# Moving three bursts of work by one step in a cosformer-attention and Swish-MLP kernel

## The chip, the cores and the metric

The kernel runs on one core of a Trainium2 chip. The metric is the device time of one execution in microseconds (us). The time before is a median of three runs. The profile is one execution on the same chip, taken apart from the timed ones. Its span, 275.6 us, runs from the first to the last recorded instruction and is shorter than the device time of that execution (277.38 us).

## What is computed

There are 8 batches of 8 heads, 576 positions and 64 features. For each batch and head:

```
r = relu(x)                                 # for q and for k
phi(x) = [r * cos(theta), r * sin(theta)]   # theta = pi/2 * position / 576
kv  = phi(k)^T v        z = sum over positions of phi(k)
att = (phi(q) kv) / (phi(q) z + 1e-6)
```

The heads are laid side by side, which gives 4608 tokens of 512 features. These go through a two-layer network with 2048 hidden features:

```
h = x @ w_in ;  g = h * sigmoid(beta * h) ;  out = g @ w_out
```

All inputs and outputs are fp32. The kernel multiplies in bf16.

## The kernel before, in words

The tokens are handled in nine chunks of 512, the attention in eight batches of 576 positions. A batch of attention is always computed inside the chunk before the one that needs it. The order of the work is written out by hand: every engine runs its instructions in the order in which the Python code emits them, and only waits on results hold one back.

**Chunk 0** is the loop over 32 slots at L783. Slots 0 to 15 make one group of 128 hidden features each: four matmuls of 512 columns, and one Swish on ScalarE (`h_group`). Slots 16 to 31 multiply by w_out: slots 16 to 23 call `o_part(0, tt, part)`, which takes one token tile and four hidden groups; slots 24 to 31 take one hidden group for all four token tiles, `o_mm(0, tt, (slot - 16,))`. Each of these slots is four matmuls of 512 columns. Slot 24 reads row 8 of the bf16 weights, `wout[:, 8]`, slot 25 row 9, and so on. A row is made by `cast_out(j)`, on VectorE, or on ScalarE where the call has `"a"`: it copies one row from the fp32 staging tile and divides by beta.

After its matmuls, a slot calls what the dictionary `early` (L736) has for it. These are the bursts of the second batch (b = 1):

- slot 4, `rest()`: emits the VectorE work that later slots find in the queue, last of all `v_scale(1, 0)`, `k_relu(1)`, and the two halves of `q_relu` for batch 1, which need the transfer of raw q;
- slot 22: the keys-values product `kv_mm` (72 small matmuls into banks 6 and 7), and its copy `kv_take` on ScalarE;
- slot 23, `second()` (L720): 18 transposes of q on TensorE (`q_turn_pe`), then copies of them (`takes`) shared between ScalarE and VectorE, with `cast_out(8)` to `cast_out(15)` mixed in;
- slots 25 and 26, `num_seven`: the numerators, with their division on VectorE; slot 25 has `cast_out(13)` too;
- slots 28 and 29, `x_turn_pe`: the transposes of the result, and their copies.

**Chunk 1** is the loop at L811: 16 slots of `h_group(1, slot)`. Between them lie the preparations for batch 2. `v_half(2, 1, n0, n1)` multiplies positions n0 to n1 - 1 (of nine) of v by the sine: slots 3 to 8 do pieces 3 to 8 on ScalarE, slot 4 does pieces 0 to 2 on VectorE. `w_sums` (slot 6) makes four sums of weight blocks on VectorE. `kv_all(2)` (slot 11) is the keys-values product and its copy on VectorE, followed by the multiplication of q by the tangent (`tan_mul`), also on VectorE. Chunk 1 ends with the products of w_out, which use a fast scheme with seven block products for eight (`o_fast`, L536), and reads `kv` in `num_all(2, ...)` there.

**Chunk 2** (L1013 with c = 2) works likewise and ends with a list of product calls: `y["1"]`, `y["5"]` and so on are eight-step matmul products on TensorE, `y["c1"]` and the like are copies, `y["a2"]`, `y["a7"]`, `y["a3"]` are additions on VectorE. Product "4" is accumulated in the same bank (`b_ps`) that addition "a7" reads. `x_sums(3)` and `wh_sums(12)` are VectorE sums of inputs and of weights for the fast scheme of chunk 3.

Of the kernel before, what the change touches and what calls it, by code (L numbers as in the profile page):

```python
# [17 lines left out]
NQ = 9  # L18
# [4 lines left out]
def kernel(  # L23
# [93 lines left out]
    def cast_out(j, eng="d"):  # L117
        i, jj = divmod(j, 4)
        st = stages["out", i]
        if eng == "a":  # L120
            nc.scalar.activation(wout[:, j, :], st[:, jj, :], AF.Copy, scale=rbeta[:, j : j + 1])
        else:
            nc.vector.tensor_scalar(wout[:, j, :], st[:, jj, :],
                                    scalar1=rbeta[:, j : j + 1], scalar2=None, op0=ALU.mult)
# [138 lines left out]
    def kv_out(jp, bank):  # L263
        return ps[:, bank : bank + 2, jp * 2 * E : (jp + 1) * 2 * E]

    def kv_mm(b, jp, bank, jjs=(0, 1)):
        t = kv_out(jp, bank)
        for n in range(NQ):
            for jj in jjs:
                for g in range(2):  # L270
                    hs = slice(g * HP, (g + 1) * HP)
                    nc.tensor.matmul(  # L272
                        t[jj * HP : (jj + 1) * HP, g], lhsT=rk[hs, n, 2 * jp + jj, :],
                        rhs=vb[hs, n, 2 * jp + jj].rearrange("q s e -> q (s e)"),
                        start=(n == 0), stop=(n == NQ - 1))

    def kv_take(jps, bank, eng="dve"):
        a0, a1 = jps[0], jps[-1] + 1
        o = kv[:, :, a0:a1].rearrange("q g s c e -> q g (s c e)")
        a = ps[:, bank : bank + 2, a0 * 2 * E : a1 * 2 * E]  # L280
        if eng == "act":
            nc.scalar.copy(o, a)
        else:
            nc.vector.tensor_copy(o, a)
# [14 lines left out]
    def x_rden(bank, slot, n0, n1, jps):  # L299

        w, m = len(jps), n1 - n0
        nv = ps[:, bank : bank + 2, slot * E : (slot + w * m) * E].rearrange("q j (i s e) -> q j i s e", s=w, e=E)
        den = small.tile([P, 2, m, w], FP32, name="den", tag=f"den{m}{w}")
        nc.vector.tensor_tensor(  # L304
            den, nv[:, :, :, :, D],
            eps9[:, n0:n1].unsqueeze(1).unsqueeze(3).to_broadcast([P, 2, m, w]), op=ALU.add)
        rden = small.tile([P, 2, m, w], FP32, name="rden", tag=f"rden{m}{w}")
        nc.vector.reciprocal(rden, den)
        return nv, rden, n0, jps

    def x_mul(got, n0, n1):
        nv, rden, first, jps = got
        a, z, w = n0 - first, n1 - first, len(jps)
        o = xs[:, n0:n1, jps[0] : jps[-1] + 1].rearrange("q n s (j d) -> q j n s d", j=2)
        nc.vector.tensor_tensor(  # L315
            o.rearrange("q j n s d -> q j (n s) d"),
            nv[:, :, a:z, :, 0:D].rearrange("q j n s d -> q j (n s) d"),
            rden[:, :, a:z].rearrange("q j n s -> q j (n s)").unsqueeze(3).to_broadcast([P, 2, (z - a) * w, D]),
            op=ALU.mult)
# [27 lines left out]
    def x_turn_pe(b, n0, n1, bank, engs=("act",), jps=(0, 1)):  # L347
        m, w = n1 - n0, len(jps)
        tv = ps[:, bank].bitcast(BF16)[:, 0 : w * m * P].rearrange("q (n s c) -> q n s c", n=m, s=w)
        for i in range(m):  # L350
            for s_, jp in enumerate(jps):
                nc.tensor.matmul(tv[:, i, s_, :], lhsT=xs[:, n0 + i, jp, :], rhs=ident, is_transpose=True,  # L352
                                 start=(i == 0 and s_ == 0), stop=(i == m - 1 and s_ == w - 1))
        for k_, (c, o, a, z) in enumerate(pieces(b, n0, n1)):
            dst, src = xt_tile(c)[:, o : o + z - a, jps[0] : jps[-1] + 1], tv[:, a - n0 : z - n0]
            if engs[k_ % len(engs)] == "act":
                nc.scalar.copy(dst, src)
            else:
                nc.vector.tensor_copy(dst, src)
# [80 lines left out]
    def wh_sums(jt):  # L440
        f0 = jt % 4
        A11, A12, A21, A22 = (win[jt // 4][:, 2 * jp : 2 * jp + 2, f * P : (f + 1) * P]
                              for f in (f0, f0 + 1) for jp in range(2))
        s1, s2, s3, s4 = (w_sum(jt, i) for i in range(4))
        nc.vector.tensor_tensor(s1, A21, A22, op=ALU.add)
        nc.vector.tensor_tensor(s3, A11, A21, op=ALU.subtract)
        nc.vector.tensor_tensor(s2, s1, A11, op=ALU.subtract)
        return nc.vector.tensor_tensor(s4, A12, s2, op=ALU.subtract)
# [265 lines left out]
    def num_seven(jp, bank):  # L714
        for n in range(7):
            num_mm(1, n, jp, bank, n)
# [3 lines left out]
    def second():  # L720

        takes.append(q_turn_pe(1, 0, 4, hold=True))
        takes.append(q_turn_pe(1, 1, 6, hold=True))
        cast_out(8)
        takes[0]("act", 0)
        takes[0]("dve", 1)
        cast_out(9, "a")
        takes[0]("dve", 0)
        takes[0]("act", 1)
        cast_out(10)  # L730
        for e, i in (("act", 0), ("dve", 1), ("act", 1), ("dve", 0)):
            takes[1](e, i)
        for j in (11, 12, 14, 15):
            cast_out(j, "a")
# [1 line left out]
    early = {  # L736
        4: lambda: (num_mm(0, 8, 0, 2, 0), num_mm(0, 8, 1, 2, 1), rest()),
        15: lambda: v_scale(1, 1, eng="act"),
        22: lambda: (kv_mm(1, 0, 6), kv_mm(1, 1, 6), kv_take((0, 1), 6, "act")),
        23: second,  # L740
        25: lambda: (num_seven(0, 4), x_mul(x_rden(4, 0, 0, 7, (0,)), 0, 7), cast_out(13)),
        26: lambda: (num_seven(1, 6), x_mul(x_rden(6, 0, 0, 7, (1,)), 0, 7)),
        28: lambda: x_turn_pe(1, 0, 7, 4, ("act",), (0,)),
        29: lambda: x_turn_pe(1, 0, 7, 5, ("dve",), (1,)),
    }

    def num_rest():
# [14 lines left out]
    def v_half(b, cs, n0=0, n1=NQ, eng="dve"):  # L762
        if b >= B:
            return
        v_scale(b, cs, n0=n0, n1=n1, eng=eng)
        if cs == 1 and n1 == NQ and b + 1 < B:
            load_raw(b + 1, "v")
# [3 lines left out]
        if b + 1 < B:  # L771
            load_raw(b + 1, "k")

    def kv_all(b, bank=6):
        kv_mm(b, 0, bank)
        kv_mm(b, 1, bank)
        kv_take((0, 1), bank)

    def x_part(b, t, bank):
        x_div(t, bank)  # L780
# [30 lines left out]
    for slot in range(16):  # L811
        h_group(1, slot)
        if slot == 0:
            num_rest()
            att_q(2)
            v_half(2, 0)
        if 3 <= slot < NQ:
            v_half(2, 1, slot, slot + 1, "act")
        if slot == 4:
            k_all(2)  # L820
            v_half(2, 1, 0, 3)
        elif slot == 6:
            w_sums()
        elif slot == 11:
            kv_all(2)
            for jp in range(2):
                tan_mul(nc.vector, qs_of(2)[:, jp], qts[0][:, jp], 0, NQ)
    q_relu(3, 0, "act")
# [184 lines left out]
    for c in range(2, NTC):  # L1013
        b = c + 1
        parts = (6, 0, 4) if c < FAST else (0, 6, 4)
        xb, yb = ((2, 3, 6), (1 if c == FAST - 1 else 7, 3, 6)) if c < FAST else ((3, 2, 0), (1, 2, 0)) if b < B else ((0, 3, 6), (1, 3, 6) if c + 1 < NTC else (1, 4, 7))
        x, y = o_fast(c, 0, xb), o_fast(c, 1, yb)
        if c >= FAST:
            chunk(c, b, x, y, parts)
            continue  # L1020
        sums = h_first(c)
        for t, bank in enumerate(parts):
            num_all(b, t, bank)
        q_tan(b + 1, 0, sums)
        q_tan(b + 1, 1)
        for i, n in enumerate("156273"):
            x[n]()
            if n in "156":
                x["c" + ("u" if n == "6" else n)]()
                x_part(b, i, parts[i])  # L1030
        for j in range(4):
            k_piece(b + 1, j)
        for n in ("a7", "a2", "a3"):
            x[n]()
        att_q(b + 2, False)
        y["1"]()
        y["c1"]()
        v_half(b + 1, 1, 0, 1, "act")
        x["4"]()
        x["c4"]()  # L1040
        v_half(b + 1, 1, 1, 2, "act")
        v_half(b + 1, 0, 0, 5)
        y["5"]()
        y["c5"]()
        if c == FAST - 1:
            x_sums(c + 1)
            wh_sums(12)
        v_half(b + 1, 1, 2, 3, "act")
        y["6"]()
        y["cu"]()  # L1050
        y["2"]()
        y["a2"]()
        y["7"]()
        y["a7"]()
        v_half(b + 1, 0, 5, 7)
        y["3"]()
        y["a3"]()
        v_half(b + 1, 0, 7, 9)
        v_half(b + 1, 1, 3, 9, "act")
        y["4"]()  # L1060
        y["c4"]()
        q_turn_dma(b + 2)
# [30 lines left out]
```

## Time and profile before

| | before |
|---|---|
| time, median of 3 | 278.01 us (277.81 to 278.37) |
| span of the profiled execution | 275.6 us |
| TensorE matmuls | 268.9 us busy, 98% |
| VectorE | 221.0 us, 80% |
| ScalarE | 184.6 us, 67% |
| GpSimd | 67.8 us, 25% |
| TensorE clock granted | 1.00 |

The busy time of TensorE includes modelled matmul ends, so short idle times between two matmuls are better read from the start times in the timeline. The chain of waits goes back from the last instruction to what released each step; it says which engine set the end, piece by piece. In the timeline a row is a run of like instructions: start, length, engine, source line, operation, output and input tile, count, and in brackets how long the engine had been idle before and what ended that.

A 512-column matmul of chunk 0 starts 0.216 us after the one before it (eight of them from 41.28 us on take 1.89 us, the last of them 0.379 us), so a slot of four takes 0.87 us.

### The profile page before, as it was taken

Reading aid. Unit: us, or ns where it says so; the run is one execution under the profiler, and the core shown is the slowest. Engines: PE = TensorE matmul, PEld = TensorE weight load, DVE = VectorE, ACT = ScalarE, POOL = GpSimd, SP = SyncE. Lnnn points to the kernel's source line nnn. Section 1 sums busy time; section 2 is a strip of 40 time slices with the busy share of each in tenths; the row PEclk is TensorE's granted clock in tenths of the full one; section 3 lists DMA queues with packets and bytes.
Section 4 is the critical chain, followed back from the end, with each engine's and each line's share of the span. In section 5 each row is a group of like instructions: output and inputs, shape, how many; then the busy total and the mean of one; then the engine's idle time right before and its main releaser. Section 6 shows DMA issues by size and latency. Waiting matters only on the chain.

```text
span 275.6 us, 9047 instructions
## 1 busy us (share of the span) xinstructions
PE 268.9 (98%) x3749; PEld 199.8 (73%) x3749; DVE 221.0 (80%) x578; ACT 184.6 (67%) x381; POOL 67.8 (25%) x87
## 2 busy tenths in 40 slices
PE   8899999999999999999999999999999999999993
PEld 8554455446875599869866998688768886888683
DVE  5989968599999898599959995899589589558851
ACT  5778757797248657697669756976694289429821
POOL 1444000600087073106420552044300140000000
PEclk9999999999999999999999999999999999999999
DMA  7999999999969999961899199915400640033005
GB/s 248 369 394 382 393 389 312 375 193 377 244 153 309 245 309 295 394 130 38 179 359 267 39 220 301 121 21 107 114 2 12 117 115 2 0 70 86 2 24 130
DMA packets 50745, 54.00 MB, mean 196 GB/s; under 512 B 31232, under 2 KB 31760, under 8 KB 50704
## 3 DMA queue, kind: packets, MB, share of 16 engines
q1 hardware_dynamic: 47744, 45.88, 59.5%
q0 software_dynamic: 2688, 7.34, 8.9%
q8 instruction: 29, 0.48, 0.7%
q10 hardware_dynamic: 272, 0.21, 0.3%
q14 instruction: 12, 0.10, 0.2%
HBM read 36.71 MB, written 9.44 MB: 167 GB/s over the span
## 4 chain that ended last, share of the span: by engine, by line
PE 83%; DMA 12%; DVE 2%; ACT 1%; SPq 1%; issue 0%; ACTq 0%; DVEq 0%
PE ps L547 35%; PE ps L468 16%; PE ps L422 13%; PE ps L380 10%; DMA raw_q<-in_q_dram 7%; DMA w_stage<-in_moe_w_in_dram 5%; PE ps L293 4%; PE ps L517 3%; PE ps L272 2%; DVE win L115 1%; ACT vb L217 1%; SPq L79 1%; PE ps L234 0%; PE ps L352 0%; DVE qb L194 0%
## 5 line engine op out<-in xcount | busy, mean ns | idle before, releaser
L413 ACT ACTIVATE g_t<-ps,beta 128x512 bf16<-128x512 f32 x96 | 61.0, 698 | 3.1 <-DVE ps L498 2.8
L547 PEld LDWEIGHTS <-S 128*128 128x128 bf16 x589 | 51.3, 98 | 5.0
L510 POOL DMA_DIRECT2D out_dram<-o_sb x56 | 33.5, 604 | 66.3 <-ACT o_sb L523 24.6
L380 PE MATMUL ps<-xt,win 128*128 128x512 bf16 (+1 forms) x196 | 42.8, 375 | 0.1
L547 PEld LDWEIGHTS <-g_t 128*128 128x128 bf16 x440 | 38.2, 98 | 4.3 <-issue 0.3
L422 PE MATMUL ps<-xt,win 128*128 128x512 bf16 (+1 forms) x184 | 40.8, 351 | 0.0
L388 ACT ACTIVATE g_t<-ps,beta 128x512 bf16<-128x512 f32 x48 | 32.2, 690 | 8.0 <-PE ps L380 7.8
L380 PEld LDWEIGHTS <-win 128*128 128x128 bf16 x196 | 18.8, 98 | 21.0 <-issue 0.4
L547 PE MATMUL ps<-wout,g_t 128*128 128x256 bf16 (+1 forms) x284 | 31.7, 262 | 0.0
L547 PE MATMUL ps<-wout,S 128*128 128x256 bf16 (+1 forms) x305 | 31.5, 255 | 0.0
L547 PE MATMUL ps<-T,S 128*128 128x256 bf16 (+1 forms) x284 | 30.8, 262 | 0.0
L399 DVE TENSOR_TENSOR S<-g_t 128x512 bf16<-128x512 bf16 (+1 forms) x66 | 25.1, 409 | 3.6 <-ACT g_t L413 2.7
L217 ACT ACTIVATE vb<-raw_v,sin 128x256 bf16<-128x256 f32 (+1 forms) x61 | 27.4, 501 | 0.9 <-DMA raw_v<-in_v_dram 0.9
L222 POOL TENSOR_TENSOR qs<-qt,tanr 128x1152 bf16<-128x1152 bf16 x6 | 14.2, 2382 | 50.8 <-DVE den L304 29.8
L468 PEld LDWEIGHTS <-w_stage 128*128 128x128 bf16 x224 | 21.6, 98 | 6.7
L468 PE MATMUL ps<-w_stage 128*128 128x256 bf16 x168 | 26.2, 272 | 0.0
L422 PEld LDWEIGHTS <-win 128*128 128x128 bf16 x184 | 17.9, 98 | 10.1
L315 DVE TENSOR_TENSOR xs<-ps,rden 128x768 bf16<-128x768 f32 (+4 forms) x26 | 22.8, 883 | 0.8
L219 DVE TENSOR_SCALAR vb<-raw_v,cos 128x256 bf16<-128x256 f32 x63 | 20.5, 380 | 0.1
L468 PEld LDWEIGHTS <-win 128*128 128x128 bf16 x168 | 16.4, 98 | 4.8 <-issue 0.3
L468 PE MATMUL ps<-xt,win 128*128 128x256 bf16 x112 | 19.1, 273 | 0.0
L594 ACT COPY p<-ps 128x256 f32<-128x256 f32 x16 | 6.0, 373 | 17.0 <-PE ps L547 16.9
(105 smaller groups left out, 417.6 us busy)
## 6 DMA issues: line engine op xcount, KB each, us to landing
raw_v<-in_v_dram SPq DMA_DIRECT2D x7, 1152.0 KB, 9.9
raw_k<-in_k_dram SPq DMA_DIRECT2D x7, 1152.0 KB, 7.5
raw_q<-in_q_dram SPq DMA_DIRECT2D x7, 1152.0 KB, 7.7
out_dram<-o_sb POOLq DMA_DIRECT2D x56, 128.0 KB, 4.4
w_stage<-in_moe_w_in_dram SPq DMA_DIRECT2D x3, 1024.0 KB, 13.0
w_stage<-in_moe_w_out_dram SPq DMA_DIRECT2D x2, 1024.0 KB, 8.1
w_stage<-in_moe_w_out_dram SPq DMA_DIRECT2D x4, 512.0 KB, 11.9
out_dram<-o_sb SPq DMA_DIRECT2D x12, 128.0 KB, 2.4
```

What stands on the lines that cost most here:

```text
L217: nc.scalar.activation(o, a, AF.Copy, scale=t[:, n : n + 1])
L219: nc.vector.tensor_scalar(o, a, scalar1=t[:, n : n + 1], scalar2=None, op0=ALU.mult)
L222: return eng.tensor_tensor(dst.rearrange("q n (g p) -> q n g p", g=2), src.rearrange("q n (g p) -> q n g p", g=2), tanr[:, n0:n1].unsqueez ...
L315: nc.vector.tensor_tensor(o.rearrange("q j n s d -> q j (n s) d"), nv[:, :, a:z, :, 0:D].rearrange("q j n s d -> q j (n s) d"), rden[:, :, ...
L380: nc.tensor.matmul(ps[:, h_bank(c, jt), i * 64 : (i + w) * 64], lhsT=win[jt // 4][:, mi, (jt % 4) * P : (jt % 4 + 1) * P], rhs=xt[:, i : i ...
L388: nc.scalar.activation(gs[c, jt // 4][:, jt % 4], ps[:, h_bank(c, jt)], AF.Silu, scale=beta[:, jt : jt + 1])
L399: return nc.vector.tensor_tensor(o, l, r, op=op)
L413: nc.scalar.activation(gs[c, jt // 4][:, jt % 4], ps[:, bank], AF.Silu, scale=beta[:, jt : jt + 1])
L422: nc.tensor.matmul(ps[:, bank, o * 64 : z * 64], lhsT=win[jt // 4][:, mi, (jt % 4) * P : (jt % 4 + 1) * P], rhs=xt[:, o:z, jp, g * HP : (g ...
L468: nc.tensor.matmul(dst, lhsT=left[:, g], rhs=right[:, :, g * HP : (g + 1) * HP], start=start and g == 0, stop=stop and g == 1, skip_group_ ...
L510: (eng or own).dma_start(out=out_v[bb, n][:, m0:m1], in_=o_sb[hf * HP : (hf + 1) * HP, m0:m1])
L547: nc.tensor.matmul(dst[:, m : m + w], lhsT=left(i), rhs=right[:, i, m : m + w], start=start and i == 0, stop=stop and i == order[-1], skip ...
```

## The change

There are three moves. They are meant to place each burst nearer to the time at which its inputs are there and its engine is free.

1. **Chunk 0, second batch.** Each burst comes one slot later: keys-values from slot 22 to 23, `second` from 23 to 24, the numerators from 25 and 26 to 26 and 27, the transposes of the result from 28 and 29 to 29 and 30. The purpose is to give the raw transfers of batch 1 one more slot to arrive. Since slot 24 reads `wout[:, 8]`, `cast_out(8)` can no longer stand in `second`; it is emitted with the keys-values burst in slot 23.
2. **Chunk 1, keys-values.** `kv_all(2)` comes in slot 10 in place of 11, and its copy is done by ScalarE in place of VectorE. For the sine pieces to be ready sooner, VectorE makes five of them (0 to 4) and ScalarE four (5 to 8), in slots 2 to 5.
3. **Chunk 2, the sums.** `wh_sums(12)`, four VectorE additions, moves from ahead of the additions `y["a2"]`, `y["a7"]`, `y["a3"]` to behind them.

```
         takes.append(q_turn_pe(1, 0, 4, hold=True))
         takes.append(q_turn_pe(1, 1, 6, hold=True))
-        cast_out(8)
         takes[0]("act", 0)
         takes[0]("dve", 1)
         cast_out(9, "a")
...
-        22: lambda: (kv_mm(1, 0, 6), kv_mm(1, 1, 6), kv_take((0, 1), 6, "act")),
-        23: second,
-        25: lambda: (num_seven(0, 4), x_mul(x_rden(4, 0, 0, 7, (0,)), 0, 7), cast_out(13)),
-        26: lambda: (num_seven(1, 6), x_mul(x_rden(6, 0, 0, 7, (1,)), 0, 7)),
-        28: lambda: x_turn_pe(1, 0, 7, 4, ("act",), (0,)),
-        29: lambda: x_turn_pe(1, 0, 7, 5, ("dve",), (1,)),
+        23: lambda: (kv_mm(1, 0, 6), kv_mm(1, 1, 6), kv_take((0, 1), 6, "act"), cast_out(8)),
+        24: second,
+        26: lambda: (num_seven(0, 4), x_mul(x_rden(4, 0, 0, 7, (0,)), 0, 7), cast_out(13)),
+        27: lambda: (num_seven(1, 6), x_mul(x_rden(6, 0, 0, 7, (1,)), 0, 7)),
+        29: lambda: x_turn_pe(1, 0, 7, 4, ("act",), (0,)),
+        30: lambda: x_turn_pe(1, 0, 7, 5, ("dve",), (1,)),
...
-    def kv_all(b, bank=6):
+    def kv_all(b, bank=6, eng="dve"):
         kv_mm(b, 0, bank)
         kv_mm(b, 1, bank)
-        kv_take((0, 1), bank)
+        kv_take((0, 1), bank, eng)
...
-        if 3 <= slot < NQ:
-            v_half(2, 1, slot, slot + 1, "act")
+        if 2 <= slot < 6:
+            v_half(2, 1, slot + 3, slot + 4, "act")
         if slot == 4:
             k_all(2)
-            v_half(2, 1, 0, 3)
+            v_half(2, 1, 0, 5)
         elif slot == 6:
             w_sums()
-        elif slot == 11:
-            kv_all(2)
+        elif slot == 10:
+            kv_all(2, eng="act")
...
         if c == FAST - 1:
             x_sums(c + 1)
-            wh_sums(12)
         v_half(b + 1, 1, 2, 3, "act")
...
         v_half(b + 1, 0, 7, 9)
+        wh_sums(12)
         v_half(b + 1, 1, 3, 9, "act")
```

## The prediction

> **What bounds the kernel now.** I read the page first. Its row of busy times leaves TensorE as the only candidate:
>
> ```profile
> PE 268.9 (98%) x3749; PEld 199.8 (73%) x3749; DVE 221.0 (80%) x578; ACT 184.6 (67%) x381; POOL 67.8 (25%) x87
> ```
>
> At 98% no transfer or other engine can be worth much except where TensorE stands still, so next I went through the chain of waits in order of time and looked for pieces that are not TensorE's. From 40 us to the end there is one such stretch ahead of the last microsecond. These are the two places (start, length, what):
>
> ```profile
> 24.45 14.81 DMA raw_q<-in_q_dram
> 39.26 0.02 issue
> 39.28 0.77 DVE qb L194
> 40.05 0.05 issue
> 40.10 1.34 PE ps L234 x18
> 41.44 1.73 PE ps L517 x8
> ...
> 107.43 0.05 DVEq L599
> 107.48 0.21 issue
> 107.69 0.42 DVE o_sb L599
> 108.11 0.04 issue
> 108.16 1.05 PE ps L547 x15
> ```
>
> The reader is to see two things. Raw q of batch 1 lands at 39.26, VectorE takes its relu, and TensorE's transposes start 0.05 us after the first half of that. At 108.16 TensorE waits for a VectorE addition. Between 41 and 105 us TensorE sets the pace, so **every microsecond lost or won on TensorE in either place goes into the total**. The third look is the timeline around 40 us:
>
> ```profile
> 39.01 1.04 PE L517 MATMUL ps<-wout,g_t 128*128 128x512 bf16 x4
> 39.28 1.43 DVE L194 TENSOR_SCALAR qb<-raw_q 128x1152 bf16<-128x1152 f32 x2 [1.64 <-DMA raw_q<-in_q_dram]
> ...
> 40.59 0.69 ACT L239 COPY qt<-ps 128x640 bf16<-128x640 bf16 x1 [0.50 <-PE ps L234]
> 40.64 0.48 DVE L123 TENSOR_SCALAR wout<-w_stage,rbeta 128x512 bf16<-128x512 f32 x1
> ...
> 41.18 0.72 ACT L121 ACTIVATE wout<-w_stage,rbeta 128x512 bf16<-128x512 f32 x1
> ...
> 41.28 1.89 PE L517 MATMUL ps<-wout,g_t 128*128 128x512 bf16 x8
> ```
>
> Here `cast_out(8)` is the VectorE row at 40.64, directly behind q's relu, and `cast_out(9)` the ScalarE row at 41.18, behind the first copy of the transposes. They end at 41.12 and 41.90. Slots 24 and 25 (the x8) start at 41.28 and 42.15, just behind them: the 18 transposes lie in TensorE's order ahead of slot 24 and give both casts time.
>
> **What the Trainium skill says.** "PSUM — Partial Sum Buffer", section "Engine vs sequencer instructions": ScalarE's and VectorE's queues are strict FIFO, and matmuls start in program order, with weight loads alone pulled ahead. The trace agrees: VectorE sits idle for 1.64 us for raw q with `cast_out(8)` behind it in the queue. The same page, section "PSUM bank collisions raise a hardware error": instructions of two engines on one bank are kept apart, reads against reads included. Here ScalarE's copy at 43.48 came 0.51 us late, after VectorE's tangent product on the same bank. The working below rests on both.
>
> **Part 1, chunk 0.** Nothing is added or removed; the order changes. What it wins: slot 23's last matmul starts at 39.01 + 3 x 0.216 = 39.66, so TensorE could go on at 39.88 and starts the transposes at 40.10, a wait of 0.22; the second nine wait 0.16 to 0.18 for the second half of q (weight load at 40.76, "0.16 <-DVE qb" in the rows of weight loads). That is 0.40 us.
>
> What it loses, step by step. TensorE now runs slot 23 at 37.78 (28 matmuls from 31.72), keys-values at 38.7 to 39.9, and then wants slot 24. But slot 24 reads the row of `cast_out(8)`. That call has moved only behind the keys-values burst in the code; on VectorE it is still behind q's relu, which was emitted in slot 4. It cannot end before 41.12. So slot 24 starts at 41.12 + 0.05 = 41.17 and TensorE idles 1.3 us, with the transposes queued behind it although their q is there at 40.71.
> Slot 24 takes 4 x 0.216 = 0.87, so the transposes start at 42.04. ScalarE's first copy waits for them, and `cast_out(9)` is queued behind that copy. Before, the cast ended at 41.90, which is 1.80 behind the transposes' start at 40.10. With the same lag it ends at 43.84, and slot 25 starts at 43.89. The transposes are over at about 43.0, so TensorE idles 0.87 a second time. Before, slot 25 started at 42.15 with the same work done: **+1.74 us, in which the 0.40 won is already counted**.
> Slot 26 follows at 44.76; its `cast_out(10)`, on VectorE behind two tangent products of 0.70 each from about 42.8, ends at 44.6 and costs nothing. The numerators (0.58) bring TensorE to 46.3. Slot 27 needs `cast_out(11)`: behind the copies of the second nine transposes, which alternate between two engines on one bank, I get 45.2 + 0.48 + 0.71 = 46.42, so slot 27 starts at 46.47, another 0.17. Slot 28 would start at 47.33 + 0.65 for the second numerators = 48.0, against 46.09 before. Sum for part 1: **+1.9 us**. After slot 28 the casts lead: `cast_out(13)` ends at about 48.5, slot 29 starts at 48.9. The result's last copy (0.62, starting 0.59 after its transposes) has only slot 31 (0.87) and the transposes' 0.4 to hide in, and ends just in time for chunk 1.
> The bounds: if only the first wait is real, +0.87 (the transposes' 0.98 us less the 0.11 that slot 24 starts earlier). If the copies run without gaps, 1.7; if the alternation slips by one more copy (0.59), 2.5.
>
> **Part 2, chunk 1.** VectorE loses the keys-values copy (0.69) and gains two sine pieces (three took 0.87 from 57.91, so 0.58): -0.11. ScalarE loses two pieces of 0.52 and gains a copy of about 0.59. The product on TensorE, 1.15, moves by one slot and keeps its length; it had no visible wait for the sine pieces (ScalarE's last started at 59.91, the product at 61.28). VectorE's fifth piece would now end near 58.8 + 0.6, plus the shift of 1.9 that all of chunk 1 takes from part 1, 61.3; slot 10 ends at 60.35 + 1.9 = 62.25, so nothing waits. The reader of `kv`, the numerators at 67.73, also needs the tangent product, which ended at 66.71: 1 us of slack either way. ScalarE has 1.34 idle where the burst stands. I take **0**, from -0.15 to +0.2.
>
> **Part 3, chunk 2.** The VectorE rows in order:
>
> ```profile
> 106.43 0.28 DVE L445 TENSOR_TENSOR w_stage<-win 128x256 bf16<-128x256 bf16 x1
> ...
> 107.15 0.29 DVE L448 TENSOR_TENSOR w_stage<-win,w_stage 128x256 bf16<-128x256 bf16 x1
> 107.36 0.42 DVE L597 TENSOR_TENSOR o_sb<-ps,p 128x256 f32<-128x256 f32 x1
> 107.69 0.41 DVE L599 TENSOR_TENSOR o_sb<-ps,p 128x256 f32<-128x256 f32 x1
> ```
>
> The four sums hold VectorE from 106.43 to 107.36, and "a2" and "a7" queue behind them. TensorE's products "7" and "3" are 30 half-width matmuls from 106.07; at 0.058 each (a row of 15 starts 0.88 before the next) they are issued by 107.82, yet "4" starts at 108.16, after "a7" has read its bank: 0.34 us idle. Without the sums "a2" could run at 106.4 and "a7" as soon as "7" is out, at about 107.1, ending at 107.5, before 107.82. So **-0.34**. The sums then lie at about 109 to 110 in a VectorE hole (2.16 us idle before 111.64) and cost nothing; chunk 3 reads them much later.
>
> **Sum:** 1.9 + 0 - 0.34 = +1.56, so 278.01 + 1.56 = 279.57, which I give as 279.55.
>
> **Rivals.**
> - *The extra slot hides the transfer*: if the row of w_out were there when slot 24 wants it, part 1 would win its 0.40, part 3 0.34: 278.01 - 0.74 = 277.27, faster. For it: the chain does pass through raw q, and the wait is real. Against: that row stands behind the same relu, and a wait for q has been turned into a wait for something behind q. 7 in 100.
> - *Only the first wait*: `cast_out(9)` comes in time, for example since ScalarE passes its copy sooner. 278.01 + 0.87 - 0.34 = 278.54. Against: the copy needs the transposes and stands ahead of the cast in one queue. 11 in 100; it falls about evenly within 0.2% and above.
> - *The bursts collide further*: one more copy's slip in chunk 0 (+0.6), or the keys-values product in chunk 1 waiting for VectorE. 278.01 + 2.5 - 0.34 = 280.2. 8 in 100.
> - *The forecast*, both waits: 74 in 100, spread from 279.0 to 280.0 by the size of the second wait and the little third one, and by the 0.3 or so by which runs differ (277.81 to 278.37).
>
> **Range and chances.** 0.2% is 0.56 us: faster means below 277.45, slower above 278.57. Faster: the first rival, with a little for what the trace doesn't show, 0.08. Same: half of the second, 0.07. Slower: the rest, 0.85. The range reaches down to the second rival's time and up to the third's: 278.6 to 280.2.
>
> **What would show it.** In the timeline after: slot 24's w_out matmuls start about 1.3 us after the end of the keys-values product, within 0.1 of the end of `cast_out(8)`; slot 25 starts about 0.9 after the end of the 18 transposes, within 0.1 of the end of `cast_out(9)`; chunk 1 begins near 52.2 in place of 50.34. The chain should pass from raw q over q's relu and `cast_out(8)` to TensorE, and then over ScalarE's copy and cast. At chunk 2's end, "4" follows "3" without the 0.34. I am wrong if raw q lands more than a microsecond earlier than in this trace, if slot 24 starts before q's relu has ended, or if chunk 1 has waits of its own that take up the shift.

## The result, and the profile after

| | before | after |
|---|---|---|
| time, median of 4 | 278.12 us (277.81 to 278.37) | 279.88 us (278.99 to 280.1) |
| ratio of the runs after to those before | | 1.0058, 95% interval 1.0033 to 1.0082 |
| span of the profiled execution | 275.6 us | 278.3 us |
| chunk 1's first matmul | 50.34 us | 52.76 us |
| chunk 3's first matmul | 109.04 us | 111.04 us |

The change makes the kernel 1.76 us slower by the medians, 1.6 by the ratio. Two of the runs of the experiments below, one of them of the kernel before, were over 1.5% slower than the fastest of their kernel and are left out of medians and ratios. The page after gives TensorE less busy time in a longer span. The busy time alone proves nothing: it is 266.8 us in `p3_alone` below too, whose span is that of the kernel before. The second row says more:

```profile
PE 266.3 (96%) x3745; PEld 198.1 (71%) x3749; DVE 221.5 (80%) x579; ACT 184.8 (66%) x380; POOL 67.7 (24%) x87
...
L517 PE MATMUL ps<-wout,g_t 128*128 128x512 bf16 x60 | 14.7, 379 | 2.7 <-DVE wout L123 1.6
```

It is new among the costliest groups: w_out's matmuls of chunk 0, with 2.7 us of idle time just before them, most of it ended by VectorE's cast of a row. Four of these 64 matmuls are missing from the trace, one of them in slot 24, which is why a slot can show as x3. The timeline of this stretch shows where nearly all of the 2.7 lie:

```profile
38.80 1.22 PE L272 MATMUL ps<-vb,rk 64*64 64x130 bf16 x72
39.75 1.43 DVE L194 TENSOR_SCALAR qb<-raw_q 128x1152 bf16<-128x1152 f32 x2 [1.64 <-DMA raw_q<-in_q_dram]
...
41.10 0.48 DVE L123 TENSOR_SCALAR wout<-w_stage,rbeta 128x512 bf16<-128x512 f32 x1
...
41.64 1.02 PE L517 MATMUL ps<-wout,g_t 128*128 128x512 bf16 x3 [1.63 <-DVE wout L123]
...
42.50 1.17 PE L234 MATMUL ps<-ident,qb 128*128 128x128 bf16 x18
...
43.57 0.72 ACT L121 ACTIVATE wout<-w_stage,rbeta 128x512 bf16<-128x512 f32 x1
...
44.34 1.89 PE L517 MATMUL ps<-wout,g_t 128*128 128x512 bf16 x8 [0.68 <-ACT wout L121]
...
46.98 1.02 PE L517 MATMUL ps<-wout,g_t 128*128 128x512 bf16 x3 [0.17 <-ACT wout L121]
```

TensorE waits three times for a row of w_out: 1.63 us ahead of slot 24, 0.68 ahead of slot 25, 0.17 ahead of slot 27. In the chain of waits, raw q is now followed by the cast, and the transposes come after slot 24:

```profile
24.47 15.25 DMA raw_q<-in_q_dram
39.72 0.02 issue
39.75 1.43 DVE qb L194 x2
41.17 0.42 DVE wout L123
41.60 0.04 issue
41.64 0.38 PE ps L517
...
42.66 0.52 PE ps L234 x9
...
43.27 1.42 DVE qs L222 x2
44.70 0.39 DVE wout L123
45.09 0.61 DVE qs L222
45.70 0.02 issue
45.72 0.59 ACT qt L239
46.31 0.63 ACT wout L121
46.94 0.04 issue
46.98 0.38 PE ps L517
```

Behind the transposes (L234) the chain does not pass through the wait of 0.68. It goes over VectorE, two tangent products (L222), the cast of row 10 and a further product, to ScalarE's copy and the cast of row 11, and comes back to TensorE at slot 27. So the small wait of 0.17 is the one that sets the end: had slot 25 come sooner, TensorE would have stood longer ahead of a later slot.

At the end of chunk 2 the wait is gone. Addition "a7" (L599) ends at 109.94, before product "3" is through, and "4" follows at 110.15:

```profile
108.37 1.95 PE L547 MATMUL ps<-wout,S 128*128 128x256 bf16 x30
...
109.52 0.42 DVE L599 TENSOR_TENSOR o_sb<-ps,p 128x256 f32<-128x256 f32 x1 [0.37 <-PE ps L547]
...
110.15 1.05 PE L547 MATMUL ps<-T,g_t 128*128 128x256 bf16 x15
```

The two profiled spans differ by 2.7 us, and the matmul starts divide that. Raw q of batch 1 landed about 0.47 later in the execution after (its relu starts at 39.75 against 39.28), though the order of transfers up to there is the same; TensorE came to slot 16 only 0.08 later. From that relu to chunk 1 it is 13.01 against 11.06: **+1.95**, part 1. From chunk 1's first matmul to its first product of w_out it is 15.55 in both: **0**, part 2. From there to chunk 3 it is 42.73 against 43.15: **-0.42**, part 3 and a little more. From chunk 3 to the end it is about 0.7 more, most of it one pause of TensorE near 127 us that the trace gives to no other engine. 0.47 + 1.95 - 0.42 + 0.7 = 2.7.

### The profile page after: what moved, and what is told of

Same layout as the page of the kernel before. It is cut to its first block, busy times and chain, and to the rows that moved or that the text cites. A ratio compares the mean times of both kernels' runs of the same rounds, so it can differ in the third digit from the quotient of the medians.

```text
span 278.3 us, 9043 instructions
## 1 busy us (share of the span) xinstructions
PE 266.3 (96%) x3745; PEld 198.1 (71%) x3749; DVE 221.5 (80%) x579; ACT 184.8 (66%) x380; POOL 67.7 (24%) x87
## 4 chain that ended last, share of the span: by engine, by line
PE 84%; DMA 8%; DVE 3%; ACT 1%; issue 1%; SPq 0%; ACTq 0%; DVEq 0%
PE ps L547 35%; PE ps L468 16%; PE ps L422 12%; PE ps L380 12%; DMA raw_q<-in_q_dram 5%; PE ps L293 3%; DMA raw_k<-in_k_dram 3%; PE ps L272 3%; PE ps L517 2%; DVE xs L315 1%; DVE qs L222 1%; DVE qb L194 1%; SPq L79 0%; PE ps L352 0%; DVE win L115 0%
## 5 line engine op out<-in xcount | busy, mean ns | idle before, releaser
L217 ACT ACTIVATE vb<-raw_v,sin 128x256 bf16<-128x256 f32 (+1 forms) x59 | 26.3, 501 | 1.5 <-DMA raw_v<-in_v_dram 1.5
L222 POOL TENSOR_TENSOR qs<-qt,tanr 128x1152 bf16<-128x1152 bf16 x6 | 14.2, 2387 | 50.8 <-PE ps L547 36.1
L517 PE MATMUL ps<-wout,g_t 128*128 128x512 bf16 x60 | 14.7, 379 | 2.7 <-DVE wout L123 1.6
```

The costliest lines, as they stand in the source:

```text
L217: nc.scalar.activation(o, a, AF.Copy, scale=t[:, n : n + 1])
L517: nc.tensor.matmul(o_ps[:, m0 : m0 + w], lhsT=gs[c, jt // 4][:, jt % 4, tt * P : (tt + 1) * P], rhs=wout[:, jt, m0 : m0 + w], start=(jt == ...
```

## The experiments

The runs are in three groups, each compared with runs of the kernel before on the same chip: medians 278.02 (43 runs), 278.47 (47) and 278.18 (59). These runs of one and the same kernel spread from 277.14 to 279.75 in the first group alone, so a few tenths are read better from the distances inside a trace than from medians. "Relu to chunk 1" below is the distance from the start of q's relu for batch 1 to chunk 1's first matmul, "slot 16 to chunk 1" the one from the first w_out matmul of chunk 0. Each kernel has one trace, so these distances scatter too. Before, `p23_alone` and `p3_alone` have the same chunk 0; in them q's relu starts 7.56, 7.47 and 7.87 us after slot 16, and slot 16 to chunk 1 takes 18.62, 18.52 and 18.92: a raw q that lands later moves chunk 1 by as much.

**The parts one by one.** `p1_alone` has part 1 of the diff, `p3_alone` part 3, `p23_alone` parts 2 and 3.

> Only part 1 of the change (chunk 0's bursts one slot later), parts 2 and 3 as before. My theory: part 1 carries the whole loss, about +1.9 us over the kernel before, so near 280.0. Rival (the three parts interact: the loss needs chunk 1's or chunk 2's new order too): clearly less, within 0.5 us of before.

> Parts 2 and 3 without part 1. My theory: part 2 is worth nothing, part 3 wins the 0.34 us for which product 4 waited: 0.2 to 0.5 us faster than before, near 277.7. Rival (chunk 1's new order costs something that the late start of chunk 1 hid): same as before or slower.

> Part 3 alone (the four weight sums behind the additions in chunk 2). My theory: 0.3 us faster than before, and equal to parts 2 and 3 together within 0.2 us; product 4 follows product 3 without a wait. Rival: the sums collide with chunk 3's first additions and give it back, so no difference to before.

| | time | ratio to before (95%) | relu to chunk 1 | chunk 1 to its w_out | from there to chunk 3 |
|---|---|---|---|---|---|
| before | 278.02 | | 11.06 | 15.55 | 43.15 |
| p1_alone | 280.00 | 1.0076 (1.0048 to 1.0103) | 13.03 | 15.55 | 43.66 |
| p23_alone | 278.17 | 1.0010 (0.9988 to 1.0032) | 11.05 | 15.56 | 42.73 |
| p3_alone | 277.82 | 0.9992 (0.9975 to 1.0009) | 11.05 | 15.55 | 42.74 |

Part 1 alone carries the loss, 1.98 us by medians and 1.97 by the trace. (Its last stretch is 0.5 longer than before since raw v of a later batch came 0.5 us after VectorE was ready for it in that execution, ahead of the four sums.) Part 3 takes 0.42 out of chunk 2's end; the wait is gone in both kernels that have it, and "4" starts at 108.01 in `p3_alone` with "a7" ended at 107.79:

```profile
106.82 0.42 DVE L597 TENSOR_TENSOR o_sb<-ps,p 128x256 f32<-128x256 f32 x1
107.37 0.42 DVE L599 TENSOR_TENSOR o_sb<-ps,p 128x256 f32<-128x256 f32 x1
...
108.01 1.05 PE L547 MATMUL ps<-T,g_t 128*128 128x256 bf16 x15
...
109.14 0.28 DVE L445 TENSOR_TENSOR w_stage<-win 128x256 bf16<-128x256 bf16 x1
```

As time it is not proved: the interval of `p3_alone` holds both 0 and 0.42, and that of `p23_alone` lies mostly above no change and ends short of 0.42. The 0.2 to 0.5 us expected of `p23_alone` were not seen. Whether part 2 costs some tenths in executions that were not profiled stays open; in the trace its stretch is equal to 0.01 us.

**The first wait.** In `row8_from_7` slot 24 reads another row:

```
-  rhs=wout[:, jt, m0 : m0 + w],
+  rhs=wout[:, 7 if c == 0 and jt == 8 else jt, m0 : m0 + w],
```

> The changed kernel, but slot 24 reads row 7 of w_out, which is there long before, in place of row 8 (so the output has a wrong row in it); all else is as changed. This takes away the first wait and nothing else. My theory: the transposes then start about 1.2 us sooner, right behind slot 24, and everything after them with them, since their copies and casts are queued behind them: 1.2 to 1.7 us faster than the changed kernel, near 278.4. Rival (the second wait stands on its own clock, for example the transfer of rows 9 and 10): the time is given back at slot 25, at most 0.5 us faster than the changed kernel.

Measured 278.68, ratio 1.0025 (1.0002 to 1.0047). That is 0.66 us above the kernel before, where the changed kernel is 1.76 above it: 1.1 won, just under what was expected.

```profile
40.02 1.04 PE L517 MATMUL ps<-wout,g_t 128*128 128x512 bf16 x4
40.89 1.17 PE L234 MATMUL ps<-ident,qb 128*128 128x128 bf16 x18
42.73 1.89 PE L517 MATMUL ps<-wout,g_t 128*128 128x512 bf16 x8 [0.68 <-ACT wout L121]
```

From relu to slot 25 it is 3.27 in place of 4.59 after, so the transposes' whole chain came 1.32 sooner; the 0.68 ahead of slot 25 stayed as it was. So the second wait is not on a clock of its own, it follows the transposes. Relu to chunk 1 is 12.18, only 0.83 less than the 13.01 after: the other 0.5 was lost to a pause inside the second numerators.

The next run asks what slot 24 waits for. In `cast8_act`:

```
-        23: lambda: (kv_mm(1, 0, 6), kv_mm(1, 1, 6), kv_take((0, 1), 6, "act"), cast_out(8)),
+        23: lambda: (kv_mm(1, 0, 6), kv_mm(1, 1, 6), cast_out(8, "a"), kv_take((0, 1), 6, "act")),
```

> The changed kernel, with cast_out(8) given to ScalarE, which stands idle there, ahead of the keys-values copy. It takes the cast out from behind q's relu. Theory A (the prediction's: the relu in VectorE's queue holds the cast): the cast runs at about 39.9 us, slot 24 starts about 0.9 us sooner than in the changed kernel, and the time falls by 0.5 to 0.9 us. Theory B (the row's own transfer, issued behind raw q, lands only at about 41.0 us in the changed kernel's trace, so the relu's place in the queue hides behind it): the cast starts at 41.05 all the same, takes 0.71 in place of 0.48, and slot 24 starts 0.2 later: time the same or 0.2 us more than the changed kernel.

Theory B holds. ScalarE was free for 3.58 us, and the cast still did not start before 41.00, when its row had landed:

```profile
41.00 0.72 ACT L121 ACTIVATE wout<-w_stage,rbeta 128x512 bf16<-128x512 f32 x1 [3.58 <-DMA w_stage<-in_moe_w_out_dram]
...
41.78 1.02 PE L517 MATMUL ps<-wout,g_t 128*128 128x512 bf16 x3 [1.80 <-ACT wout L121]
```

The time was 280.61, 1.0068 (1.0031 to 1.0104). The first half of w_out's third tile, rows 8 and 9, is issued at 26.57 in the trace before and lands 14.0 us later, at 40.6:

```profile
L101 SPq DMA_DIRECT2D w_stage<-in_moe_w_out_dram x1: 3324/3324/3324, 26.6 to 26.6; - x1
...
DMA to landing us min/median/max: 14.0/14.0/14.0
```

Raw q, issued ahead of it, lands at 39.26, and its relu ends at 40.7. In the changed kernel the rows land at about 41.05 (14.3 us after 26.75), the relu ends at 41.18, and the cast starts at 41.10. Queue and transfer let the cast go within about 0.1 us of each other, and taking it out of the queue alone wins nothing. `row8_first` keeps this edit and changes the transfer too; the new last argument of `load_w` picks rows 8 and 9 (0) or rows 10 and 11 (2):

```
-  load_raw(1, "q")
-  load_w("out", 2, 2)
+  load_w("out", 2, 2, 0)
+  load_raw(1, "q")
+  load_w("out", 2, 2, 2)
```

> As the run with cast_out(8) on ScalarE, and the transfer of rows 8 and 9 is issued ahead of raw q of batch 1 in place of behind it. Both theories of the first wait: slot 24 now starts right behind the keys-values product, with no wait. Raw q lands some 1.3 us later (0.5 MB at the 390 GB/s of this stretch), so the transposes wait for it: they start about 0.6 us sooner than in the changed kernel. The second wait stays at 0.87 behind the transposes. Time 0.4 to 0.8 us below the changed kernel, and still above the kernel before.

Measured 279.48, 1.0036 (1.0016 to 1.0057). The w_out matmuls follow the keys-values product without a wait, and the transposes stand 0.3 us behind them for raw q:

```profile
39.74 1.04 PE L517 MATMUL ps<-wout,g_t 128*128 128x512 bf16 x3
40.91 1.34 PE L234 MATMUL ps<-ident,qb 128*128 128x128 bf16 x18
```

Slot 16 to chunk 1 is 19.59, against 20.96 after and 18.62 before: 1.37 of the 2.34 between these two is gone. The kernel is still slower than before: slot 25 starts 1.86 us behind the start of the transposes, as in the changed kernel (1.84), with 0.51 of it idle.

**The second wait.** `cast9_ahead` takes `cast_out(9)` from its later place in `second` and puts it ahead of the copies, the first of the added lines below; `casts_ahead` has all three, each taken from its later place:

```
   takes.append(q_turn_pe(1, 1, 6, hold=True))
+  cast_out(9, "a")
+  cast_out(10)
+  cast_out(11, "a")
   takes[0]("act", 0)
```

> The changed kernel, with cast_out(9) alone emitted ahead of the copies. My theory of a row of casts behind copies: slot 25 starts 0.87 sooner, but slot 26 then waits for cast_out(10), which is behind two tangent products on VectorE and ends where it ended in the changed kernel: the gain is given back at once, 0 to 0.2 us faster than the changed kernel. Rival (cast_out(9) is the only late one): 0.8 us faster.

> The changed kernel, with cast_out(9), (10) and (11) emitted ahead of the copies of the transposes, so that they no longer stand behind them. My theory: the first wait stays (1.6 us idle ahead of slot 24); slot 25 follows the transposes without the 0.87 wait, slot 27 without its 0.17; about 1.0 us faster than the changed kernel. Rival (the copies, pushed back by the casts, hold the numerators instead): a new wait ahead of the first numerators takes half or more of it back, at most 0.5 us faster.

`cast9_ahead`: 280.40, 1.0060 (1.0033 to 1.0088); relu to chunk 1 is 13.02, as in the changed kernel (13.01). Slot 25 did come sooner, and slot 26 gave it back, which the timeline shows as a new wait for the next row:

```profile
43.37 1.03 PE L517 MATMUL ps<-wout,g_t 128*128 128x512 bf16 x4
...
44.48 0.48 DVE L123 TENSOR_SCALAR wout<-w_stage,rbeta 128x512 bf16<-128x512 f32 x1
...
45.01 1.02 PE L517 MATMUL ps<-wout,g_t 128*128 128x512 bf16 x4 [0.61 <-DVE wout L123]
...
46.85 1.02 PE L517 MATMUL ps<-wout,g_t 128*128 128x512 bf16 x3 [0.24 <-ACT wout L121]
```

The two waits, 0.61 and 0.24, add up to the 0.68 and 0.17 after, 0.85 both times, as the chain of the changed kernel has it: slot 27 is held by the cast of row 11 whatever slot 25 does.

`casts_ahead`: 279.12, 1.0018 (0.9998 to 1.0039); relu to chunk 1 is 11.95, 1.06 less than after. Slots 25 and 26 follow the transposes as one row of eight without a bracket:

```profile
41.09 1.02 PE L517 MATMUL ps<-wout,g_t 128*128 128x512 bf16 x3 [0.93 <-DVE wout L123]
...
41.95 1.17 PE L234 MATMUL ps<-ident,qb 128*128 128x128 bf16 x18
...
42.95 1.89 PE L517 MATMUL ps<-wout,g_t 128*128 128x512 bf16 x8
```

The first wait, which this edit does not touch, is 0.93 here and 1.63 after: raw q's relu starts 7.25 us after slot 16 here and 7.95 there, the same 0.70 apart.

**Both waits away, and raw q in halves.** `both_fixed` is `row8_first` with `casts_ahead`. `both_fixed_q` splits raw q of batch 1 into two transfers besides, and puts `cast_out(11)` behind the second copy on ScalarE. `p23_qhalves` is `p23_alone` with the split of raw q alone.

> The changed kernel with both waits of chunk 0 taken away together: rows 8 and 9 transferred ahead of raw q with cast_out(8) on ScalarE, and casts 9 to 11 emitted ahead of the copies. My theory: the two waits are the whole loss of part 1, so chunk 0 ends where it did in the kernel before within 0.3 us (a wait for raw q of some 0.5 us stays ahead of the transposes), and with part 3's gain the time is 0.1 to 0.6 us below the kernel before. Rival (part 1 has a third cost, for example in the burst of the result's transposes, which has one slot less to hide in): 0.5 us or more above that.

> As the kernel with both waits taken away, and raw q of batch 1 comes in two transfers of half the size, so that the first half's relu need not wait for the second; cast_out(11) goes behind the second copy on ScalarE. My theory: the transposes too start with no wait, TensorE has no idle time over 0.1 us in chunk 0's second half, and chunk 0 ends about 0.4 us sooner than in the kernel before; with part 3's 0.4 about 0.8 us below the kernel before, the fastest of all. Rival (the stretch is bound by its transfers, so the wait comes back at another row of w_out): chunk 0 ends no sooner than in the kernel before.

> Parts 2 and 3 without part 1, and raw q in two transfers of half the size. My theory (from the landing of row 8 at 40.6 us in the trace of before): the transposes start some 0.2 to 0.4 us sooner than without the split, but slot 24 then waits for the cast of row 8, which cannot end before 41.1, so chunk 0 ends only about 0.1 us sooner. Rival (raw q alone sets the pace here): chunk 0 ends 0.4 us sooner.

| | time | ratio to before (95%) | slot 16 to chunk 1 |
|---|---|---|---|
| before | 278.18 | | 18.62 |
| p23_alone (first group) | 278.17 | 1.0010 (0.9988 to 1.0032) | 18.52 |
| both_fixed | 278.66 | 1.0028 (1.0009 to 1.0047) | 19.38 |
| both_fixed_q | 278.68 | 1.0016 (0.9999 to 1.0034) | 19.43 |
| p23_qhalves | 277.61 | 0.9974 (0.9952 to 0.9997) | 18.21 |

The two that were to repair part 1 missed. In the trace `both_fixed` ends chunk 0 later than before, by 0.76 us. TensorE waits for raw q ahead of the transposes in both kernels, and that costs only 0.08 more here. The other 0.68 lies in the second numerators, from slot 27 to slot 28, where TensorE pauses and the trace names nothing:

```profile
46.45 0.22 PE L293 MATMUL ps<-kv,qt 64*64 64x65 bf16 x3 [0.47 <-issue]
```

(The bracket counts from the modelled end of a matmul and so shows less than the distance between starts.) So this trace shows no third cost of part 1 but the pause. The timed runs, with part 3's gain included, are 0.48 us above the kernel before by the medians: something is still lost, and whether such pauses make it up stays open. In `both_fixed_q` the transposes start on time (40.55, right behind slot 24), but they take 1.48 us in place of 1.17, since raw q's second half comes late, and the new order of casts and copies makes TensorE wait 0.34 for the last tangent product and 0.26 for `cast_out(13)`. Whether a third order would be free stays open.

`p23_qhalves` is the only one whose interval lies below the kernel before, by 0.57 us in the medians. Its upper end, 0.9997, is close to no change, and it is one of eleven kernels tried, so this is a sign and not a proof. Its transposes start at 40.31 right behind slot 23 and run as one row without the two waits for q, and slot 16 to chunk 1 is 0.41 shorter than before, which is what the rival said. The expected stop at slot 24 did not show: in this execution TensorE came to slot 16 0.44 later than before, and the cast of row 8 ended at 41.12, ahead of slot 24 at 41.32. So this trace doesn't tell which of the two theories sets the limit when TensorE comes sooner. It does show once more what the cast waits for. The relu of q's second half ended at 40.02, and VectorE then stood idle until row 8 had landed:

```profile
40.63 0.49 DVE L123 TENSOR_SCALAR wout<-w_stage,rbeta 128x512 bf16<-128x512 f32 x1 [0.61 <-DMA w_stage<-in_moe_w_out_dram]
```

## Why the prediction was right, and where its reasons were not

- **The sum.** 1.56 us slower was forecast, 1.76 measured by the medians; both lie well within the interval of the ratio (0.9 to 2.3 us). The two stretches of the trace that the change moved give 1.95 - 0.42 = 1.53.
- **First wait.** Forecast: 1.3 us idle ahead of slot 24, which starts 0.05 behind the cast of row 8. Measured: 1.63, with a start 0.06 behind the cast (41.58 to 41.64). The excess is raw q's later landing: with the relu 7.56 us after slot 16, as before, in place of 7.95, the wait would be 1.24 (an estimate from these two traces; `p1_alone`, at 7.78, has 1.47). The size held. **The step that failed is its reason**: the prediction put the cast's time down to its place behind q's relu alone and never asked when the row had landed. As a sign that the queue holds the cast it named the 1.64 us in which VectorE stood idle for raw q, but in the trace before the row landed only at 40.6, after that idle time. `cast8_act` and `p23_qhalves` show that the transfer holds the row until about the same moment. The number came out because before's cast had started right then, with the end of the relu and the landing 0.1 us apart: so far it was luck, and a mending built on the reason given, another engine for the cast, won nothing.
- **Second wait.** Forecast: slot 25 1.85 behind the start of the transposes. Measured 1.84, in the changed kernel and in `row8_from_7` alike. The rival that `cast9_ahead` stood for, one late cast, is out: moving it shifted the wait to the next rows. The path failed here: the chain was to go on over ScalarE's first copy and the cast of row 9, and it goes over VectorE's products and the cast of row 10 to the cast of row 11.
- **Third wait.** 0.17 forecast, 0.17 measured, ahead of slot 27. The prediction called it little; it is the one that ends last. The sum does not suffer, since the forecast of slot 27's start was worked out from the cast of row 11 in any case. All of part 1: 1.9 forecast, 1.95 to 1.97 by the traces.
- **Part 2** at nothing: 15.55 us on both sides in the trace.
- **Part 3** at -0.34: the wait before product "4" is gone, and the stretch is 0.42 shorter. The timed runs are too scattered to show it.
- **Rivals.** "The extra slot hides the transfer" fell because the next thing that TensorE wants is in the very next transfer. "Only the first wait" fell to the second's 0.68.
- **Rules used.** From the Trainium skill the prediction drew on two sections of "PSUM — Partial Sum Buffer". The traces agree with the strict order of each queue ("Engine vs sequencer instructions"): with `cast_out(9)` behind the copy in ScalarE's queue, slot 25 kept its 1.84 us behind the transposes. They agree too that instructions of two engines on one bank wait for each other ("PSUM bank collisions raise a hardware error"; by that page the program has to keep them apart, since the hardware does not stall): in `casts_ahead` the second copy on ScalarE stood 0.24 us for VectorE's tangent product.

## What to carry to other kernels

Before a burst is moved away from a late transfer, look at what the engine will want in its place. If that comes in the next transfer, or is made behind the same work, the wait is not hidden: here 0.40 us of waits for q became 1.63 for a row of w_out, and the burst then queued behind it. A cast that stands just ahead of its reader is on the path, so moving its reader's neighbours moves it too. Where several casts in a row are late, look for the last one in the chain: moving the first alone won nothing here. And an instruction that starts without idle time behind another may still have been held by a transfer that landed at that very moment: read the landing as well as the queue before naming the cause.

## What the runs showed of the hardware

TensorE pauses inside the bursts of 64x64 matmuls for the numerators, at different places in different profiles, and the trace names no engine or transfer for it:

```profile
127.25 0.11 PEld L293 LDWEIGHTS <-w_stage 64*64 64x64 bf16 x2 [0.62 <-issue]
```

```profile
98.45 0.22 PE L293 MATMUL ps<-kv,qt 64*64 64x65 bf16 x2 [1.08 <-issue]
```

```profile
184.27 0.23 PE L293 MATMUL ps<-kv,w_stage 64*64 64x65 bf16 x4 [1.17 <-issue]
```

These are the changed kernel, `row8_from_7` and `cast8_act`. Six of the thirteen profiles have such a pause of 0.25 us or more; before, `p1_alone`, `p23_alone`, `p3_alone`, `casts_ahead`, `cast9_ahead` and `p23_qhalves` have none. The pauses are as large as the effects sought here. Their cause was not tried, and what share they have in the spread of 277.1 to 279.8 us for one kernel is not shown.

The time at which transfers land differs from one execution to the next, and TensorE's time goes with it: by 0.4 us for raw q of batch 1 in three kernels with the same chunk 0. In the profiled execution of `casts_ahead`, raw q of a later batch came 1.3 us after ScalarE was ready for it in chunk 1, and TensorE lost 1.46 us there.
